# Prefix sums of a bucket sort on VectorE: adds with two bf16 operands become adds that take a float32 row or a PSUM scratch

## The chip, the cores and the metric

The kernel runs on one core of a Trainium2 chip. Times are device microseconds of one execution. The engines are named as the profile names them: PE (matmuls), PEld (its weight loads), DVE (VectorE), ACT (ScalarE), POOL (GpSimd, which here issues the indirect DMAs), SP (the queue of the plain DMAs).

## What is computed

One layer of message passing over a graph of 12,500 nodes with 64 features and 800,000 edges with 16 features each:

```python
def reference(x, e_attr, src, dst, w_msg, w_upd):
    N, D = x.shape
    m_in = jnp.concatenate([x[src], x[dst], e_attr], axis=-1)
    msg = _silu(m_in @ w_msg)
    agg = _segment_sum(msg, dst, N)
    return _silu(jnp.concatenate([x, agg], axis=-1) @ w_upd)
```

The edges come in random order. The kernel sorts them into 128 buckets of 98 destination nodes, and then works bucket by bucket.

## The kernel before

**Tables.** At the start `tables` multiplies the nodes with the two node parts of `w_msg`. The source part goes to DRAM as `A_d`, the destination part stays in SBUF as `BW`, one block for each bucket, with the edge part of the weights below it.

**Sorting, a step of eight tiles.** A tile is 128 edges, one on each partition. A `Step` takes M = 8 tiles, in two halves of ZB = 4. `Step.onehot` (ACT) makes `hf`, a float32 one-hot row of 128 buckets for each edge and tile. `Step.sums` (DVE, L397 to L408) adds these rows up over the tiles into `G[:, a, k, :]`, in bf16: for the half a, entry k is the sum of its tiles 0 to k. `Step.count` (PE) turns `hf` and `G` into counts, by products with triangular and all-ones matrices, into the PSUM tile `z`. `Step.ranks` (DVE, L429) reads from it each edge's place among the edges of its bucket in the chunk. `Step.expand` (DVE, L438 to L442) compares the places with slot numbers into `hit` and writes each edge's record into its slot of `X`; `Step.move` (PE, L459, then ACT, L464) sums the records of a chunk into the block `blk`, one row for each bucket. `Chunk.place` (DVE, L477, L478) moves the pointers on, and `Chunk.scatter` (POOL, L482) writes the block to DRAM with one indirect DMA.

**Chunks and turns.** The first K8 = 140 chunks have 8 tiles, one step each (`c.turn` = 3). From then on a chunk has C = 12 tiles, so that three steps hold two chunks, and `c.turn` runs through 0, 1, 2. There are 782 steps: 140 of turn 3, and 214 each of the turns 0, 1 and 2. In a chunk of 12 tiles a half can begin with tiles of its chunk already counted. The sum of these is the carry, `c.before(a)`: for the half a = 1 it is entry 3 of half 0 of the same step, for a = 0 it is entry 3 of half 1 of the step before. Entry 3 of a half is needed only where the chunk goes on after it. In turn 0 that is so for both halves, and half 1 takes a carry; in turn 1 for half 1, which begins a chunk; in turn 2 for half 0, with a carry; in turn 3 for half 0, without one.

**Messages, a batch of eight tiles.** Once enough sorted records lie in DRAM, a `Group` loads 64 tiles of them by plain DMAs, and a `Batch` of 8 tiles takes `gather` (POOL, L645: one indirect DMA for each tile, which reads 128 row numbers from `sidx` in SBUF and fetches 128 rows of `A_d` into one of four buffers `g`), `onehot` (DVE, L655, from `ioB`), `transpose` and `product` (PE, L664 and L673), `message` (DVE, L677: adds the product to the gathered rows, and so waits for the gathers; then ACT, L678), `reduce` (PE, L694) and `add` (DVE, L706).

**Order.** Every engine's queue is in the order in which `period` writes it. One period holds one stage each of a few steps and batches: the gathers of a batch with a scatter between their halves; `onehot` of a step and of the batch; the counts of the step before; the transposes; the reduction of an older batch; the ranks; `message` of an older batch; `add`; `sums` of the newest step; `expand` of the one before; `move`; the product; `place`. So on DVE a period runs L655, L429, L677, L706 twice, L403 twice, L405, L408 (in turns 0 and 2), L438, L439, L442 four times, L477, L478. POOL takes the gathers of a batch two periods before `message` needs them.

**Scratch in PSUM.** The tile `cb` is one bank of PSUM, 512 float32 wide on each partition. Before the change its columns 0 to 127 hold `ioB` (bucket-local node numbers, of which L655 reads 98), 128 to 157 `ioS`, and 256 to 495 `hit`.

Of the kernel before, what the change touches and what calls it, by code (L numbers as in the profile page):

```python
# [7 lines left out]
OP = mybir.AluOpType  # L8
# [6 lines left out]
P = 128  # L15
NBK = 128
BK = 98
# [5 lines left out]
M = 8  # L23
# [3 lines left out]
S = LIM[-1]  # L27
# [21 lines left out]
def mpnn_kernel(tc, x, e_attr, src, dst, w_msg, w_upd, out):  # L49
    nc = tc.nc  # L50
# [22 lines left out]
    with es:  # L73
# [22 lines left out]
        iof = cp.tile([P, P], F32, name="iof")  # L96
# [23 lines left out]


        cb = pc.tile([P, 512], F32, name="cb")
        ioB = cb[:, 0:P]
        ioS = cb[:, P:P + S]
        hit = cb[:, 2 * P:2 * P + M * S].rearrange("p (k s) -> p k s", s=S)
        nc.vector.tensor_copy(ioB, iof)
        nc.vector.tensor_scalar(out=ioS, in0=iof[:, 0:S], scalar1=RK, scalar2=None, op0=OP.add)


# [247 lines left out]
        class Step:  # L377
# [12 lines left out]
            def onehot(c):  # L390
                c.hf = hp.tile([P, M, NBK], F32, name="hf")

                for k in range(M):
                    nc.scalar.activation(c.hf[:, k, :], iof, AF.Square, bias=c.hi[:, k:k + 1])  # L394
                nc.scalar.activation(c.hf, c.hf, AF.Relu, bias=ones, scale=-1.0)  # L395

            def sums(c):  # L397

                c.G = tp.tile([P, 2, ZB, NBK], BF16, name="G")
                h = c.hf.rearrange("p (a k) b -> p a k b", k=ZB)  # L400
                nc.scalar.activation(c.G[:, :, 0, :], h[:, :, 0, :], AF.Copy)
                for k in (1, 2):
                    nc.vector.tensor_tensor(out=c.G[:, :, k, :], in0=h[:, :, 0, :] if k == 1 else c.G[:, :, k - 1, :], in1=h[:, :, k, :], op=OP.add)  # L403
                a, b = ((0, 2), (1, 2), (0, 1), (0, 1))[c.turn]
                nc.vector.tensor_tensor(out=c.G[:, a:b, 3, :], in0=c.G[:, a:b, 2, :], in1=h[:, a:b, 3, :], op=OP.add)  # L405
                if c.turn in (0, 2):
                    a = 1 if c.turn == 0 else 0
                    nc.vector.tensor_tensor(out=c.G[:, a, 3, :], in0=c.before(a), in1=c.G[:, a, 3, :], op=OP.add)  # L408

            def before(c, a):  # L410

# [204 lines left out]
        class Batch:  # L616
# [35 lines left out]
            def onehot(t):  # L652
                i0, n = t.i0, t.n
                t.q = qp.tile([P, BT, KQ], F32, name="q")
                nc.vector.tensor_tensor(out=t.q[:, 0:n, 0:BK], in0=ioB[:, None, 0:BK].to_broadcast([P, n, BK]), in1=t.grp.lo[:, i0:i0 + n, None].to_broadcast([P, n, BK]), op=OP.is_equal)  # L655
                nc.scalar.activation(t.q[:, 0:n, BK:KQ], t.grp.rt[:, i0:i0 + n, 0:DE], AF.Copy)

            def transpose(t, step):
# [109 lines left out]
        class Draws:  # L768
# [34 lines left out]
            def take(d, u, units):  # L803
                for f, done in zip(d.free(u), d.done):
                    left = units
                    for b in range(NB):
                        n = min(f[b], left)
                        done[b] += n
                        left -= n
# [118 lines left out]
        for k in range(0, NCH, 512):  # L928
            n = min(512, NCH - k)
# [8 lines left out]
        while work["used"] < large or (work["forming"] and work["forming"][-1].k < 2):  # L938
            b = take()
# [66 lines left out]
        while work["used"] < whole or lasts or work["cur"] is not None or work["forming"]:  # L1006
            b = take()
# [47 lines left out]
        with tc.If(more > 0):  # L1055
# [4 lines left out]
            with tc.If(nover > 0):  # L1060
# [12 lines left out]
                for k in range(0, NCH, P):  # L1073
                    n = min(P, NCH - k)
# [13 lines left out]
                with tc.For_i(0, nover, 1):  # L1088
# [36 lines left out]
                    def block(rs=None):  # L1125
                        for c in halves:
                            c.expand(rs)
                            e = c.move()
                        return e


                    c = block()
# [4 lines left out]
                    with tc.For_i(0, rounds, 1):  # L1137
                        c = block(rs)
# [36 lines left out]
```

## Time and profile before

| | us |
|---|---|
| runs of the kernel before | 8925.74, 8929.77, 8931.5 (median 8929.77) |
| the profiled execution, its time | 8929.85 |
| the span of its trace | 8928.0 |
| DVE busy in the span | 7216.6 |
| ACT busy | 5054.3 |
| POOL busy | 6599.6 |

How to read a profile of this kind: a busy time counts the engine's instructions alone. POOL's issue of an indirect DMA is shown as some 0.94 us of work and 0.30 us in which it is idle and waits for nothing that the profile shows, and this pair repeats. A row of a view that groups instructions gives line, engine, operation, output and inputs, shapes, count, then busy time and mean length, then the idle time of the engine just before them with what ended it. A row of the timeline gives the start and the length of one instruction, both in us from the start of the span. A row of a view by windows gives a stretch, its length, and for each engine the busy time in it with the number of instructions.

### The profile page before, as it was taken

To read this page: it belongs to the slowest core of one execution; us is meant where nothing else is said; L and a number is where in the kernel's file an instruction comes from. 1 tells how busy PE (TensorE), PEld (TensorE's weight loads), DVE (VectorE), ACT (ScalarE), POOL (GpSimd) and SP (SyncE) were. 2 spreads that over 40 slices of the span, in tenths; PEclk is the share of its full clock that TensorE was granted. 3 is DMA by queue.
4 is the path that set the end of the run, shared out by engine and by line. 5 is a ranking of instruction groups with operands and counts; after the bars stand their busy time and mean duration, and the time that the engine had idled before them with its cause. 6 is when DMAs were issued, how large, how long until landed. Compare 5 with 4: busy or idle time off the path is not lost. (4 is left out here: it accounts for less than half of the span.)

```text
span 8928.0 us, 155380 instructions
## 1 busy us (share of the span) xinstructions
PE 8156.2 (91%) x49053; PEld 5873.2 (66%) x49816; DVE 7216.6 (81%) x15722; ACT 5054.3 (57%) x12594; POOL 6599.6 (74%) x6908
## 2 busy tenths in 40 slices
PE   8899999999999999999999999999999999999767
PEld 5677776666666666666666666666666666666656
DVE  8999998888888888888888888888888888887233
ACT  7666666555555555555555555555555555555222
POOL 1677777777777777777777777777777777777776
PEclk9999999999999999999999999999999999999566
DMA  4222222222222222222222222222222222222323
GB/s 109 56 62 60 60 61 58 50 57 54 54 56 50 57 52 56 52 56 52 56 52 56 56 52 52 55 57 52 56 52 56 52 56 55 52 57 49 59 48 51
DMA packets 662901, 501.14 MB, mean 56 GB/s; under 512 B 492983, under 2 KB 529911, under 8 KB 662071
## 3 DMA queue, kind: packets, MB, share of 16 engines
q0 software_dynamic: 238976, 349.72, 16.8%
q1 hardware_dynamic: 422775, 141.27, 7.3%
q8 instruction: 401, 6.57, 0.3%
q14 instruction: 429, 3.51, 0.1%
q10 hardware_dynamic: 320, 0.07, 0.0%
HBM read 330.05 MB, written 152.30 MB: 54 GB/s over the span
## 5 line engine op out<-in xcount | busy, mean ns | idle before, releaser
L645 POOL DMA_INDIRECT g<-A_d,sidx x6322 | 6020.1, 952 | 1946.6 <-issue 1546.2
L459 PE MATMUL pl<-X,hf 128*128 128x291 f32 (+5 forms) x12512 | 4255.3, 492 | 6.2 <-DVE LOST L477 6.2
L459 PEld LDWEIGHTS pl<-X,hf 128*128 128x128 f32 x12512 | 2389.5, 198 | 1333.1 <-issue 842.5
L442 DVE TENSOR_TENSOR X<-cb,rec 128x442 f32<-128x442 f32 (+5 forms) x3128 | 2646.9, 908 | 26.7
L394 ACT ACTIVATE hf<-iof,shi 128x128 f32<-128x128 f32 x6256 | 1908.3, 389 | 872.9 <-PE pl L459 872.6
L673 PEld LDWEIGHTS pre<-w,qt 114*128 114x128 f32 x10496 | 1338.1, 202 | 580.7 <-issue 562.8
L673 PE MATMUL pre<-w,qt 114*128 114x64 f32 x10496 | 1343.6, 284 | 249.0 <-DVE g L677 247.3
L677 DVE TENSOR_TENSOR g<-pre,g 128x512 f32<-128x512 f32 (+1 forms) x818 | 548.9, 671 | 1191.7 <-DMA g<-A_d,sidx 769.4
L678 ACT ACTIVATE g<-g 128x512 f32<-128x512 f32 (+1 forms) x818 | 501.6, 613 | 1761.5 <-DVE g L677 1759.7
L694 PE MATMUL ag<-q,g 128*64 128x98 f32 x12644 | 775.8, 264 | 250.4 <-DVE wl L549 146.1
L429 DVE TENSOR_REDUCE rank<-z 128x8 f32<-128x1024 f32 x782 | 949.1, 1214 | 57.3 <-PE z L424 36.3
L395 ACT ACTIVATE hf<-hf,ones 128x1024 f32<-128x1024 f32 x782 | 899.1, 1150 | 25.4
L667 ACT ACTIVATE qt<-tq 114x1024 f32<-114x1024 f32 (+1 forms) x818 | 797.2, 975 | 156.5 <-PE tq L664 154.2
L664 PE MATMUL tq<-ident,q 128*114 128x128 f32 x6322 | 871.5, 283 | 14.3 <-ACT nodes L194 13.0
L694 PEld LDWEIGHTS ag<-q,g 128*64 128x64 f32 x12644 | 613.3, 143 | 411.5 <-issue 200.6
L664 PEld LDWEIGHTS tq<-ident,q 128*114 128x114 f32 x6322 | 766.9, 140 | 136.5 <-ACT nodes L194 20.5
L482 POOL DMA_INDIRECT st<-blk,ptrs x567 | 572.9, 1010 | 321.2 <-issue 141.1
L655 DVE TENSOR_TENSOR q<-cb,lo 128x784 f32<-128x784 f32 (+1 forms) x818 | 767.4, 938 | 2.2
L464 ACT ACTIVATE blk<-pl 128x512 f32<-128x512 f32 (+1 forms) x568 | 323.8, 570 | 782.9 <-PE pl L459 609.7
L706 DVE TENSOR_TENSOR ACC<-ag,ACC 64x98 f32 x1938 | 497.5, 257 | 108.6 <-PE ag L694 28.8
L422 PE MATMUL z<-G,onesb 128*128 128x384 bf16 x1564 | 511.4, 327 | 73.5 <-DVE G L403 13.7
L673 PE MATMUL pre<-BW,qt 114*128 (+1 forms) x2148 | 311.8, 305 | 109.4 <-DVE g L677 108.6
(137 smaller groups left out, 5099.1 us busy)
## 6 DMA issues: line engine op xcount, KB each, us to landing
g<-A_d,sidx POOLq DMA_INDIRECT x6322
ea<-in_e_attr SPq DMA_DIRECT2D x260, 192.0 KB
rt<-st SPq DMA_DIRECT2D x1312, 34.0 KB
st<-blk,ptrs POOLq DMA_INDIRECT x567
rt<-st SPq DMA_DIRECT2D x434, 8.5 KB
nodes<-in_x SPq DMA_DIRECT2D x62, 98.0 KB
ACC<-rt SPq DMA_DIRECT2D x11, 544.0 KB
rt<-st SPq DMA_DIRECT2D x320, 17.0 KB
```

Of the source, the lines that this page charges most:

```text
L394: nc.scalar.activation(c.hf[:, k, :], iof, AF.Square, bias=c.hi[:, k:k + 1])
L395: nc.scalar.activation(c.hf, c.hf, AF.Relu, bias=ones, scale=-1.0)
L429: nc.vector.tensor_reduce(out=c.rank, in_=c.z, axis=AX.X, op=OP.max)
L442: nc.vector.tensor_tensor(out=c.x[:, k:k + 2, 2:2 + n * R].rearrange("p k (s c) -> p k s c", c=R), in0=hit[:, k:k + 2, 0:n, None].to_broad ...
L459: nc.tensor.matmul(pl[:, 0:w], c.hf[:, k, :], c.x[:, k, 0:w], start=(n == (c.size - 1 if whole else 0)), stop=ends, skip_group_check=True)
L482: i = nc.gpsimd.indirect_dma_start(out=st, out_offset=bass.IndirectOffsetOnAxis(ap=c.ptr, axis=0), in_=c.blk[:, 2:], in_offset=None)
L645: j = nc.gpsimd.indirect_dma_start(out=t.g[:, i, :], out_offset=None, in_=A_d, in_offset=bass.IndirectOffsetOnAxis(ap=t.grp.sidx[:, k:k + ...
L655: nc.vector.tensor_tensor(out=t.q[:, 0:n, 0:BK], in0=ioB[:, None, 0:BK].to_broadcast([P, n, BK]), in1=t.grp.lo[:, i0:i0 + n, None].to_broa ...
L664: nc.tensor.transpose(t.tq[0:KQ, j * P:(j + 1) * P], t.q[:, j, :], ident)
L667: nc.scalar.activation(t.qt[:, 0:w], t.tq[0:KQ, 0:w], AF.Copy)
L673: nc.tensor.matmul(t.pre[:, i * D:(i + 1) * D], t.qt[:, i * P:(i + 1) * P], w, start=True, stop=True)
L694: o = nc.tensor.matmul(t.ag[t.half(v), v // 2 * BK:(v // 2 + 1) * BK], t.g[:, i, :], t.q[:, i, 0:BK], start=(k == 0), stop=(k == u - 1))
```

## The change

Only `Step.sums`, the layout of `cb` and the one reader of `ioB` are touched.

```diff
-        ioB = cb[:, 0:P]
-        ioS = cb[:, P:P + S]
-        hit = cb[:, 2 * P:2 * P + M * S].rearrange("p (k s) -> p k s", s=S)
-        nc.vector.tensor_copy(ioB, iof)
+        ioB = cb[:, 0:BK]
+        ioS = cb[:, BK:BK + S]
+        hit = cb[:, P:P + M * S].rearrange("p (k s) -> p k s", s=S)
+        nc.vector.tensor_copy(ioB, iof[:, 0:BK])
+        Gs = cb[:, P + M * S:2 * P + M * S]
...
-                a, b = ((0, 2), (1, 2), (0, 1), (0, 1))[c.turn]
-                nc.vector.tensor_tensor(out=c.G[:, a:b, 3, :], in0=c.G[:, a:b, 2, :], in1=h[:, a:b, 3, :], op=OP.add)
-                if c.turn in (0, 2):
-                    a = 1 if c.turn == 0 else 0
-                    nc.vector.tensor_tensor(out=c.G[:, a, 3, :], in0=c.before(a), in1=c.G[:, a, 3, :], op=OP.add)
+                for a in ((0, 1), (1,), (0,), (0,))[c.turn]:
+                    k = c.G[:, a, 2, :]
+                    if a == (1 if c.turn == 0 else 0) and c.turn in (0, 2):
+                        nc.vector.tensor_tensor(out=Gs, in0=c.before(a), in1=h[:, a, 3, :], op=OP.add)
+                        nc.vector.tensor_tensor(out=c.G[:, a, 3, :], in0=Gs, in1=k, op=OP.add)
+                    else:
+                        nc.vector.tensor_tensor(out=c.G[:, a, 3, :], in0=k, in1=h[:, a, 3, :], op=OP.add)
...
-                nc.vector.tensor_tensor(out=t.q[:, 0:n, 0:BK], in0=ioB[:, None, 0:BK].to_broadcast([P, n, BK]), in1=t.grp.lo[:, i0:i0 + n, None].to_broadcast([P, n, BK]), op=OP.is_equal)
+                nc.vector.tensor_tensor(out=t.q[:, 0:n, 0:BK], in0=ioB[:, None, :].to_broadcast([P, n, BK]), in1=t.grp.lo[:, i0:i0 + n, None].to_broadcast([P, n, BK]), op=OP.is_equal)
```

In turn 0 entry 3 was made by two adds: one over both halves (256 elements, a bf16 and a float32 operand), and one of 128 elements that adds the carry, with two bf16 operands. Now there are three of 128 elements: entry 3 of half 0; the carry plus the float32 row of half 1's last tile, into the float32 scratch `Gs` in PSUM; and `Gs` plus the sum of the half's first three tiles. In turn 2 the two adds stay two: the carry plus the float32 row into `Gs`, and `Gs` plus the sum. The instructions of turns 1 and 3 are the same as before. `ioS` and `hit` move to lower columns of the same bank, so that `Gs` has room.

## The prediction

> **What bounds the kernel now.** I read the page first, then the busy time by windows, then the waits of single engines, and last the timeline around the lines that change.
>
> ```profile
> span 8928.0 us, 155380 instructions
> PE 8156.2 (91%) x49053; PEld 5873.2 (66%) x49816; DVE 7216.6 (81%) x15722; ACT 5054.3 (57%) x12594; POOL 6599.6 (74%) x6908
> L645 POOL DMA_INDIRECT g<-A_d,sidx x6322 | 6020.1, 952 | 1946.6 <-issue 1546.2
> ```
>
> By busy share PE looks like the bound and POOL is only third. The windows over POOL say otherwise:
>
> ```profile
> 4000.00:6000.00 2000.00, 1516.65 (x1587) 0.97 0.23 54
> ```
>
> 1587 indirect DMAs leave 2000 - 1516.65 = 483.35 us idle, 0.305 us for each. That is the pause that the timeline below shows after every one of them, even with the next ready. So POOL never waits for another engine here: the gathers and scatters stand back to back, 1.25 us apart, and the kernel goes at their pace. DVE does wait, for the gathers' data (L677, from 1228 to 8250 us):
>
> ```profile
> L677 DVE TENSOR_TENSOR g<-pre,g 128x512 f32<-128x512 f32 x637 | 440.3, 691 | 899.6 <-DMA g<-A_d,sidx 587.0 <-issue 312.2
> ```
>
> 899.6 us over 637 periods is 1.41 us of slack in each. An edit on DVE is therefore worth only what it does to POOL's pace. The change touches turns 0 and 2 alone, which have one L408 each:
>
> ```profile
> L408 DVE TENSOR_TENSOR G<-G x428: 224/225/231, 1228.7 to 8212.9; 128x128 bf16<-128x128 bf16 x143
> ```
>
> So what counts lies between 1228.7 and 8212.9 us; a saving on POOL there moves everything behind it forward by as much, since POOL's gathers run on to 8906 us.
>
> **Where the two engines touch.** A gather behind which no sorting runs, and one in the sorted stretch:
>
> ```profile
> 4000.00:6000.00 2000.00, 1394.70 (x1465) 0.97 0.23 54
> 8300.00:8600.00 300.00, 226.80 (x241) 0.60 0.33 57
> ```
>
> 226.80/241 is 0.941 us for a gather in the tail, 1394.70/1465 is 0.952 us with sorting beside it: 0.011 us more in the mean. It is not spread evenly. This is a turn 0:
>
> ```profile
> 3010.46 0.94 POOL L645 DMA_INDIRECT g<-A_d,sidx  x1 [0.30 <-issue]
> 3011.71 1.16 POOL L645 DMA_INDIRECT g<-A_d,sidx  x1 [0.30 <-DMA g<-A_d,sidx]
> ...
> 3009.39 0.69 DVE L677 TENSOR_TENSOR g<-pre,g 128x512 f32<-128x512 f32 x1 [0.61 <-DMA g<-A_d,sidx]
> ...
> 3011.62 0.43 DVE L405 TENSOR_TENSOR G<-G,hf 128x256 bf16<-128x256 bf16 x1
> 3012.09 0.23 DVE L408 TENSOR_TENSOR G<-G 128x128 bf16<-128x128 bf16 x1
> 3012.23 0.17 DVE L438 TENSOR_TENSOR X<-rank,limc 128x8 f32<-128x8 f32 x1
> ```
>
> The gather of 3011.71 takes 1.16 us, 0.22 more than 0.94. L405 ends at 3012.05, 0.34 us after the gather's start. I read it so: some 0.12 us after its start (0.34 - 0.22) the gather reads its row numbers from SBUF, and where a VectorE add with both operands in SBUF is under way, it waits for that add's end. The converse happens too:
>
> ```profile
> 3043.33 0.46 DVE L403 TENSOR_TENSOR G<-hf 128x256 bf16<-128x256 f32 x1
> ...
> 3043.34 0.94 POOL L645 DMA_INDIRECT g<-A_d,sidx  x1 [0.30 <-issue]
> ```
>
> Here the gather starts 0.01 us after the add, is not lengthened, and the add takes 0.46 instead of 0.43. At 3011.62 against 3011.71, 0.09 us apart, the add won; the border lies between, and I take 0.04. L677, L706, L439 and L442 each have an operand in PSUM; the gather of 3010.46, which runs beside L677 and L706, keeps its 0.94.
>
> Turn 0 is hit most. Its chain of adds starts a fixed time after L677, L677 starts when a gather's data land, and so L405 meets a gather at nearly the same phase each time. Of the 214 turns 0, L405 lengthens a gather in 135. The windows laid on just these gathers, first those lengthened by over 0.13 us, then the others (first and last row, and the sum):
>
> ```profile
> 1404.52:1405.64 1.12, 1.12 (x1) 1.00 0.22 44
> 8190.77:8191.86 1.09, 1.09 (x1) 0.94 0.18 30
> sum 114.55, POOL 114.55; mean POOL 1.13
> ...
> 1568.53:1569.56 1.03, 1.03 (x1) 0.75 0.19 32
> 7829.76:7830.83 1.07, 1.07 (x1) 1.00 0.44 92
> sum 34.66, POOL 34.66; mean POOL 1.02
> ```
>
> The first group has 101 gathers, the second 34. Above 0.941 each they took 114.55 - 101 x 0.941 = 19.5 us and 34.66 - 34 x 0.941 = 2.7 us. The same for the 22 gathers of turns 0 that one of the two adds of L403 lengthens, and for all 147 that an add of L403 or L405 lengthens in turns 1 and 2:
>
> ```profile
> 1255.41:1256.46 1.05, 1.05 (x1) 1.00 0.71 230
> 8025.36:8026.51 1.16, 1.16 (x1) 1.00 0.13 28
> sum 23.73, POOL 23.73; mean POOL 1.08
> ...
> 1265.50:1266.46 0.96, 0.96 (x1) 1.00 0.46 153
> 8212.33:8213.32 0.99, 0.99 (x1) 1.00 0.13 31
> sum 151.33, POOL 151.32; mean POOL 1.03
> ```
>
> These are 23.73 - 22 x 0.941 = 3.0 us and 151.32 - 147 x 0.941 = 13.0 us.
>
> **The change, part by part.** The durations, from 1228 to 8250 us:
>
> ```profile
> L405 DVE TENSOR_TENSOR G<-G,hf 128x128 bf16<-128x128 bf16 x428 | 127.5, 298 | 14.7
> L405 DVE TENSOR_TENSOR G<-G,hf 128x256 bf16<-128x256 bf16 x214 | 92.1, 430 | 7.4
> L408 DVE TENSOR_TENSOR G<-G 128x128 bf16<-128x128 bf16 x428 | 96.4, 225 | 14.7
> L439 DVE TENSOR_TENSOR cb<-cb,rank 128x240 f32<-128x240 f32 x643 | 267.7, 416 | 8.4
> L706 DVE TENSOR_TENSOR ACC<-ag,ACC 64x98 f32 x1295 | 333.5, 258 | 56.4 <-issue 6.5 <-DVE g L677 1.3 <-PE pl L459 0.8
> ```
>
> *Turn 0, the wide add becomes a narrow one.* 430 ns become 298: the add begins where it did and ends 0.132 us sooner. Each of the 101 gathers that waited longer than that for its end saves 0.132, 13.3 us together; the 34 others start their read behind its end and save their 2.7 us. Sum 16.0 us. This is the whole of the gain that I can price.
>
> *Turn 0, the carry through the scratch (the first of two adds).* It has two SBUF operands and can itself hold up a gather. Its price is not in the trace. From below, L405's narrow form with like operands, 298; with L439, which writes PSUM, 416 less 112 elements at (430-298)/128 ns, it is 300. I take 298. From above 430, as if each element took twice as long. It starts 0.33 us behind the narrow add, 1.25 us into the chain, one gather's distance. A gather that it holds up, 0.04 to 0.18 us into it, thus follows one that started 0.04 to 0.17 us into the first L403; those are among the 22 above, and the wait is at most 298 - 40 - 120 = 0.14 us. Between nothing and 3 us; I take 0.4 us lost.
>
> *Turn 0, scratch plus sum.* One operand is in PSUM, as in L706, so it holds up nothing. L706's 258 plus 30 elements more makes 289 ns.
>
> *Turn 2.* The first add has the place and the operands' kind of the old L405, 298 ns; the second now has a PSUM operand and no longer holds up a gather, but the old L408, 225 long, hardly could: only one starting 40 to 105 ns into it. I take nothing. If the scratch add needed 430 ns, turn 2 would come to be what turn 0 was with its wide add, and lose some 16 us: the gain would be gone.
>
> *DVE's own time.* Behind L405 came L408 and L438, 0.61 us from L405 to L438 in the turn 0 above. After, two starts of 0.33 us and the last one 0.21:
>
> ```profile
> 3023.12 0.29 DVE L405 TENSOR_TENSOR G<-G,hf 128x128 bf16<-128x128 bf16 x1
> 3023.33 0.17 DVE L438 TENSOR_TENSOR X<-rank,limc 128x8 f32<-128x8 f32 x1
> ```
>
> That makes 0.87, 0.26 us more; in turn 2 it is 0.33 + 0.21 = 0.54 against 0.47 (3033.42 to 3033.89 below), 0.07 more. Behind it on DVE stand L438 to L478, and for these PE's moves, ACT's copy and the scatter. 214 x 0.33 = 71 us of DVE work in all, which I cost at nothing: the wait of 1.41 us ahead of L677 takes it in. If that cover were gone, it would be 71 us.
>
> *Layout of `cb`.* Columns move within one bank that DVE alone uses; the copy of `ioB` runs once. Nothing.
>
> **Sum.** 16.0 - 0.4 = 15.6 us, 8929.85 - 15.6 = 8914.3 us; the profiled execution lies 0.08 us above the median of the runs, so nothing is to be corrected. I predict 8914.
>
> **Rivals.** *The add with two bf16 operands is what blocks.* L408 takes 225 ns where L405 takes 298 for as many elements, so it runs in a faster mode, and it is what the change removes everywhere. If its mode held POOL up, all that turn 0 loses would vanish, 19.5 + 2.7 + 3.0 = 25 us, and of the 13.0 us of turns 1 and 2 some part: 8892 to 8905, say 8899. [...] The trace does not agree; a turn 2:
>
> ```profile
> 3033.28 0.94 POOL L645 DMA_INDIRECT g<-A_d,sidx  x1 [0.30 <-DMA g<-A_d,sidx]
> ...
> 3033.42 0.29 DVE L405 TENSOR_TENSOR G<-G,hf 128x128 bf16<-128x128 bf16 x1
> 3033.74 0.23 DVE L408 TENSOR_TENSOR G<-G 128x128 bf16<-128x128 bf16 x1
> 3033.89 0.16 DVE L438 TENSOR_TENSOR X<-rank,limc 128x8 f32<-128x8 f32 x1
> ```
>
> L408 lies wholly inside this gather, which keeps its 0.94; and at 3011.71 the delay ended with L405, before L408 began; turn 1 has no L408, and gathers are lengthened in it too. Chance 0.07.
>
> *The phase does not hold.* If the longer chain changes when L677 starts, gathers would meet the adds at any phase. Then an add of length d costs (d - 0.16)²/(2 x 1.25) in the mean: in turn 0 the wide add's 0.029 and L408's 0.002 become two narrow ones of 0.008, a gain of 0.015 x 214 = 3.3 us, 8926. For it: a later DVE could shift landings. Against it: L677 waits for data that POOL's pace sets. Chance 0.13.
>
> *The longer chain comes on the path.* Slower: if L677 no longer waits, every turn 0 and 2 pays for itself, 71 - 15.6 = 55 us, 8985. It decides from the point where the 0.26 us exceed L677's wait (0.61 us even in the short one above) so often that POOL finds its four buffers occupied. No pause of POOL speaks for it. Chance 0.13.
>
> **How the numbers follow.** The forecast has 0.67. Within it the gain is 15.6 give or take 4. A change of under 0.2%, 17.9 us here, is about what a measurement of this kernel can hardly tell from none. Of the forecast 0.32 lies beyond it and 0.35 within; the blocking bf16 add gives 0.07 faster, the lost phase 0.12 within, the longer chain 0.13 slower and 0.01 of the lost phase. Faster 0.39, same 0.47, slower 0.14. The range goes from the bf16 rival, 8899, to a scratch add of 430 ns, which leaves 8930, with 2 us for the spread of the runs: 8898 to 8932. Outside it lie the longer chain and a part of the bf16 rival, some 0.16.
>
> **What would show it.** Right: POOL still idles 0.305 us behind each DMA; in turn 0 the gathers that meet the third add are at most some 0.13 us longer than 0.94; the mean gather from 4000 to 6000 us falls from 0.952 to about 0.949; the scratch add takes about 298 ns and L677 still waits for gathers. Wrong: a scratch add of well over 300 ns, gathers held up beside the last add with its PSUM operand, a POOL pause over 0.4 us, or another phase of L677 against the gathers.

## The result and the profile after

Over 22 runs the changed kernel took 8913.85 us in the median (8909.3 to 8928.35), the kernel before in its 22 runs 8930.86 (8925.74 to 8934.1). The ratio is 0.9982, with a 95% interval of 0.9975 to 0.9988: 17.0 us less.

The page of the changed kernel:

```profile
span 8926.6 us, 155594 instructions
PE 8140.7 (91%) x49053; PEld 5860.1 (66%) x49816; DVE 7239.5 (81%) x15936; ACT 5057.0 (57%) x12594; POOL 6596.0 (74%) x6908
L648 POOL DMA_INDIRECT g<-A_d,sidx x6322 | 6016.1, 952 | 1949.0 <-issue 1541.8
```

This execution is the slowest of the 22, 8928.35 us, and by its span alone nothing seems gained. The reason is in the shortest and the median length of a gather, here first in the kernel before and then in the changed one (instructions of one line; min/median/max in ns, first and last start):

```profile
L645 POOL DMA_INDIRECT g<-A_d,sidx x6322: 940/944/1342, 203.4 to 8906.5; - x198
```

```profile
L648 POOL DMA_INDIRECT g<-A_d,sidx x6322: 941/947/1307, 205.7 to 8905.8; - x198
```

The median gather, which meets nothing, is 3 ns longer in this execution. 6322 x 0.003 us is 19 us, more than what separates the execution from the median of the runs (14.5 us). In f2_wide_kept and f4_reorder_after below, which have the same scratch add and last add, the median gather is 944 again; so the 3 ns belong to that execution and not to the change. What the change did is therefore read inside the execution, against its own 0.947.

POOL still stands back to back. The windows over all of its instructions, and then over the gathers alone:

```profile
4000.00:6000.00 2000.00, 1515.83 (x1588) 0.97 0.23 54
...
4000.00:6000.00 2000.00, 1393.56 (x1466) 0.97 0.23 54
```

(2000 - 1515.83)/1588 is 0.305 us of pause, as before. The mean gather is 1393.56/1466 = 0.951 us, which is 0.004 over the 0.947 of this execution's median; before it was 0.952, 0.008 over 0.944.

The adds and the wait for the gathers, from 1228 to 8250 us, grouped by line and shape:

```profile
L680 DVE TENSOR_TENSOR g<-pre,g 128x512 f32<-128x512 f32 x637 | 440.2, 691 | 874.9 <-DMA g<-A_d,sidx 559.9 <-issue 314.6
...
L408 DVE TENSOR_TENSOR cb<-G,hf 128x128 f32<-128x128 bf16 x428 | 127.2, 297 | 7.3
L411 DVE TENSOR_TENSOR G<-G,hf 128x128 bf16<-128x128 bf16 x428 | 127.2, 297 | 14.7
L409 DVE TENSOR_TENSOR G<-cb,G 128x128 bf16<-128x128 f32 x428 | 124.7, 291 | 14.7
```

L411 is entry 3 without a carry, L408 the scratch add, L409 scratch plus sum. L680 (L677 of before) still waits for gathers, 874.9/637 = 1.37 us a period.

A turn 0 in the changed kernel, DVE and then POOL:

```profile
3012.31 0.42 DVE L404 TENSOR_TENSOR G<-G,hf 128x256 bf16<-128x256 bf16 x1
3012.77 0.29 DVE L411 TENSOR_TENSOR G<-G,hf 128x128 bf16<-128x128 bf16 x1
3013.09 0.30 DVE L408 TENSOR_TENSOR cb<-G,hf 128x128 f32<-128x128 bf16 x1
3013.42 0.29 DVE L409 TENSOR_TENSOR G<-cb,G 128x128 bf16<-128x128 f32 x1
3013.63 0.16 DVE L441 TENSOR_TENSOR X<-rank,limc 128x8 f32<-128x8 f32 x1
...
3012.90 0.98 POOL L648 DMA_INDIRECT g<-A_d,sidx  x1 [0.30 <-DMA g<-A_d,sidx]
3014.18 1.00 POOL L485 DMA_INDIRECT st<-blk,ptrs  x1 [0.30 <-issue]
```

The gather starts 0.13 us into L411 and is lengthened, as the old one was by L405; but L411 is over 0.29 us after its start, and so the gather loses 0.03 us where the one quoted before lost 0.22. L411 lengthens a gather in 96 turns 0. The windows on these gathers, first, last and sum:

```profile
1232.14:1233.16 1.02, 1.02 (x1) 1.00 0.77 229
8188.62:8189.65 1.03, 1.03 (x1) 1.00 0.22 48
sum 96.90, POOL 96.90; mean POOL 1.01
```

96.90 - 96 x 0.947 = 6.0 us. The wide add cost 22.2 us by the prediction's 0.941, and 21.8 by the median of 0.944: 114.55 + 34.66 - 135 x 0.944. From L411 to L441 it is 0.86 us, 0.25 more than from L405 to L438 before.

### The profile page after: what moved, and what is told of

It is laid out like the page before. It is cut to its first block, busy times and chain, and to the rows that moved or that the text cites. A ratio compares the mean times of both kernels' runs of the same rounds, so it can differ in the third digit from the quotient of the medians.

```text
span 8926.6 us, 155594 instructions
## 1 busy us (share of the span) xinstructions
PE 8140.7 (91%) x49053; PEld 5860.1 (66%) x49816; DVE 7239.5 (81%) x15936; ACT 5057.0 (57%) x12594; POOL 6596.0 (74%) x6908
## 5 line engine op out<-in xcount | busy, mean ns | idle before, releaser
L680 DVE TENSOR_TENSOR g<-pre,g 128x512 f32<-128x512 f32 (+1 forms) x818 | 548.9, 671 | 1170.9 <-DMA g<-A_d,sidx 781.1
L681 ACT ACTIVATE g<-g 128x512 f32<-128x512 f32 (+1 forms) x818 | 501.6, 613 | 1724.0 <-DVE g L680 1720.4
```

## The experiments

The theory: POOL's pace sets the time; a gather reads its row numbers some 0.12 us after its start, and if an add with two SBUF operands is under way then, it waits for that add's end; the change gains because turn 0's wide add, which lengthened a gather in 135 of 214 turns 0, becomes one that is 132 ns shorter (430 and 298 ns before). The 0.12 us are an estimate from the trace of the kernel before: those 135 gathers end 0.82 us behind the add's end, and an undisturbed one takes 0.944. That it is the reading of the row numbers that waits is the author's reading; no trace shows what a gather does inside its 0.94 us. Below, a gather's "read" is the moment 0.12 us after its start. The main rival: the add with two bf16 operands is what blocks. A second one: the longer chain of adds has a price.

Six kernels were run, each on two chips. On the chip of the runs with e and g in their names the kernel before itself took 10,813 and 10,830 us, and POOL's pace was not its bound (the trace of e1_split below), so that these runs answer another question. Times in us, each beside runs of the kernel before on the same chip:

| kernel | time | before | difference | ratio, 95% interval |
|---|---|---|---|---|
| e1_split | 10817.73 | 10812.7 | +5.0 | 1.0005, 0.9996 to 1.0014 |
| e2_wide_kept | 10805.08 | 10812.7 | -7.6 | 0.9996, 0.9987 to 1.0005 |
| e3_reorder_before | 10795.13 | 10812.7 | -17.6 | 0.9988, 0.9978 to 0.9997 |
| e4_reorder_after | 10803.28 | 10812.7 | -9.4 | 0.9995, 0.9986 to 1.0004 |
| f1_split | 8919.64 | 8932.89 | -13.3 | 0.9984, 0.9975 to 0.9993 |
| f2_wide_kept | 8928.16 | 8932.89 | -4.7 | 0.9996, 0.9987 to 1.0005 |
| f3_reorder_before | 8908.74 | 8932.89 | -24.2 | 0.9974, 0.9965 to 0.9984 |
| f4_reorder_after | 8906.62 | 8932.89 | -26.3 | 0.9971, 0.9960 to 0.9982 |
| g5_all_wide | 10824.37 | 10830.0 | -5.6 | 0.9998, 0.9989 to 1.0006 |
| g6_long_chain | 10883.41 | 10830.0 | +53.4 | 1.0055, 1.0042 to 1.0068 |
| h5_all_wide | 8966.28 | 8942.28 | +24.0 | 1.0027, 1.0016 to 1.0037 |
| h6_long_chain | 8927.87 | 8942.28 | -14.4 | 0.9983, 0.9974 to 0.9992 |

### The wide add split, the bf16 carry kept

```diff
-                nc.vector.tensor_tensor(out=c.G[:, a:b, 3, :], in0=c.G[:, a:b, 2, :], in1=h[:, a:b, 3, :], op=OP.add)
+                for k in range(a, b):
+                    nc.vector.tensor_tensor(out=c.G[:, k, 3, :], in0=c.G[:, k, 2, :], in1=h[:, k, 3, :], op=OP.add)
```

> The kernel before, with one edit: turn 0 makes entry 3 of its two halves by two adds of 128 elements in place of one of 256; the carry is still added by an add with two bf16 operands, and there is no scratch. Theory (a gather that comes while an add with two SBUF operands is under way waits for that add's end, and the wide add of turn 0 is the one met most): nearly the whole gain is here, 16 us less than before, 8913 to 8917, and the gathers beside turn 0's adds lose some 9 us in all in place of 25. Rival (the add with two bf16 operands blocks): no gain, 8929 to 8932.

On the slower chip the difference of +5.0 us cannot be told from none, and the trace of e1_split shows why the gathers' length could not matter there. The waits of POOL from 1228 to 8250 us (waited for: total, times, longest), and DVE's add of the gathered rows (L678 there) in the same stretch:

```profile
POOL g L646 <- issue: 1133.1, 3465, 9.1
POOL g L646 <- remote: 960.1, 423, 3.2
...
L678 DVE TENSOR_TENSOR g<-pre,g 128x512 f32<-128x512 f32 x504 | 343.2, 681 | 0.0
```

POOL pauses for some 2.3 us (960.1/423) in most batches, and the add of the gathered rows is never waited into: its idle time is 0.0. The gathers are early there, and DVE would not notice one that is 0.2 us longer. There was next to nothing to shorten either: in g5_all_wide, on the same chip and with turn 0 as before, the wide add of turn 0 lengthens 3 gathers, by 0.1 us in all. "remote" means that the profile does not know what ended the pause, and what makes that chip slower is open.

> The same kernel as e1_split, on another chip: on the first one the kernel before took 10812.7 us and POOL had pauses of some 2.4 us in most batches, so POOL's pace set nothing there. Where the kernel before takes some 8930 us, theory: 8913 to 8917, and turn 0's adds cost the gathers beside them some 9 us in all in place of 25. Rival (the add with two bf16 operands blocks): 8929 to 8932.

f1_split took 8919.64 us, 13.3 less than the kernel before: without the scratch and with the bf16 add in place the larger part of the change's 17.0 is there (two comparisons, each with its own runs of the kernel before). The time is 3 us above the band of the theory. Windows on the 84 gathers that a narrow add lengthens in turns 0:

```profile
1230.51:1231.57 1.06, 1.06 (x1) 1.00 0.76 224
8083.65:8084.65 0.99, 0.99 (x1) 1.00 0.16 33
sum 83.95, POOL 83.95; mean POOL 1.00
```

83.95 - 84 x 0.944 = 4.7 us there. With the gathers that meet turn 0's first two adds all of turn 0 loses 12.7 us, not the 9 of the expectation.

### The wide add kept, no bf16 add left

```diff
                 for a in ((0, 1), (1,), (0,), (0,))[c.turn]:
                     k = c.G[:, a, 2, :]
+                    if c.turn == 0 and a == 0:
+                        nc.vector.tensor_tensor(out=c.G[:, :, 3, :], in0=c.G[:, :, 2, :], in1=h[:, :, 3, :], op=OP.add)
+                        continue
```

> The changed kernel, with one edit: turn 0 keeps the wide add of 256 elements over both halves; the scratch add and the last add then write half 1's entry again. No add has two bf16 operands any more. Theory: the gathers wait for the wide add as before, so the gain of turn 0 is gone: 8927 to 8932. Rival (the add with two bf16 operands blocks): its removal is what gains, so 8905 to 8915, as fast as the change or faster.

On the slower chip the difference of -7.6 us cannot be told from none.

> The same kernel as e2_wide_kept, on another chip. Where the kernel before takes some 8930 us, theory (the wide add of turn 0 is what the gathers wait for): 8927 to 8932. Rival (the add with two bf16 operands blocks, and none is left here): 8905 to 8915.

f2_wide_kept took 8928.16 us, with an interval that includes no change: what the theory gives, and far from the rival's 8905 to 8915. The 145 gathers that the wide add lengthens in turns 0 of f2_wide_kept:

```profile
1255.24:1256.28 1.03, 1.03 (x1) 1.00 0.51 98
8187.44:8188.48 1.03, 1.03 (x1) 1.00 0.13 32
sum 155.62, POOL 155.62; mean POOL 1.07
```

155.62 - 145 x 0.944 = 18.7 us, four times the 4.7 of the narrow add on the same chip. The rival falls. So does the new layout of `cb` as a source of the gain, since f2 has it too. The 4.7 us that the median lies below the kernel before may be noise or a small part of the change's gain (13.3 + 4.7 = 18.0, the change has 17.0); the interval does not tell them apart.

### The same adds at another time

Here `expand` is cut in two: `slots` holds the two instructions of L438 and L439, which find each edge's slot, and runs between the adds that make entries 1 and 2 and those that make entry 3. Every add is as it was. First in the kernel before, then in the changed one:

```diff
+                if between:
+                    between.slots()
                 a, b = ((0, 2), (1, 2), (0, 1), (0, 1))[c.turn]
...
-                h.sums()
+                h.sums(z)
```

> The kernel before, with the two small instructions that find each edge's slot (limit and hit, one SBUF operand that counts) moved ahead of the add or adds that make entry 3; every add stays as it was, wide and bf16 ones too. Entry 3 begins some 0.4 us later against L677. Theory: the phase at which a gather's read meets the chain is what costs; gathers cluster 0.95 to 1.2 us behind the chain's start, where now no add with two SBUF operands runs. Of the 38 us lost beside the adds some 9 remain: 8930 - 29 = 8901, between 8896 and 8910. Rival (what the operands are decides, not when they run): no change, 8929 to 8932.

> The same kernel as e3_reorder_before, on another chip. Where the kernel before takes some 8930 us, theory (the phase at which a gather's read meets the chain decides): 8896 to 8910, with every add as before. Rival (what the operands are decides): 8929 to 8932.

f3_reorder_before took 8908.74 us, 24.2 less than the kernel before, within the band, with the wide add and the bf16 add both in place. That is more than the 17.0 of the change, though the two were not timed side by side and their intervals overlap. A turn 0 of f3_reorder_before, DVE and then POOL:

```profile
3074.68 0.42 DVE L404 TENSOR_TENSOR G<-G,hf 128x256 bf16<-128x256 bf16 x1
3075.02 0.17 DVE L441 TENSOR_TENSOR X<-rank,limc 128x8 f32<-128x8 f32 x1
3075.20 0.42 DVE L442 TENSOR_TENSOR cb<-cb,rank 128x240 f32<-128x240 f32 x1
3075.53 0.41 DVE L408 TENSOR_TENSOR G<-G,hf 128x256 bf16<-128x256 bf16 x1
...
3075.39 0.94 POOL L652 DMA_INDIRECT g<-A_d,sidx  x1 [0.30 <-DMA g<-A_d,sidx]
```

The gather starts 0.19 us into L442, which has an operand in PSUM; the wide add starts 0.14 us behind the gather, after its read, and the gather keeps its 0.94 us. The wide add (L408 there) still lengthens 36 gathers in turns 0, but the windows on these sum to

```profile
sum 35.66, POOL 35.66; mean POOL 0.99
```

which is 35.66 - 36 x 0.944 = 1.7 us in all. The expectation left some 9 us lost; counted over all adds of `sums` in turns 0 to 2 it is 17.9, most of it beside the first two adds. (It also gave both moved instructions one SBUF operand that counts; L441 has both of its operands in SBUF, of 8 elements, and took 0.17 us above.)

On the slower chip the same kernel was 17.6 us faster, at an interval that just leaves out no change. Since POOL paces nothing there, the theory has no reason for it. It may be that X is begun earlier; no run here shows it. So the move may bring something of its own on the other chip too: the gathers account for 19.7 of the 24.2 us (table below).

> The changed kernel with the same move of the two small instructions ahead of the adds that make entry 3. Theory: some 9 us remain lost beside the adds, as in the kernel before with that move, so 8898 to 8906, some 13 us faster than the change, and equal to the other kernel with the move within 3 us: with the phase out of the way the change's own edits are worth next to nothing. Rival (operand types decide): 8914, no gain over the change.

On the slower chip the difference of -9.4 us cannot be told from none.

> The same kernel as e4_reorder_after, on another chip. Where the kernel before takes some 8930 us, theory: 8898 to 8906, within 3 us of the kernel before with the same move. Rival (operand types decide): 8914.

f4_reorder_after took 8906.62 us, 0.6 above the band, within 2.1 us of the kernel before with the same move, as the theory has it, and the fastest kernel of this study. It was not timed beside the change itself: against the kernel before it gains 26.3 us and the change 17.0, and the two intervals overlap by a little. In its turns 0 the third add lengthens no gather, and the scratch add one; what is left, 13.1 us over turns 0 to 2 where some 9 were expected, is lost almost wholly beside the first two adds.

### Longer adds in turns 1 and 2

```diff
-                a, b = ((0, 2), (1, 2), (0, 1), (0, 1))[c.turn]
+                a, b = ((0, 2), (0, 2), (0, 2), (0, 1))[c.turn]
```

> The kernel before, with turns 1 and 2 also taking the add over both halves (256 elements in place of 128; the entry made in vain is read by nobody). Theory (a gather waits for the end of the add that its read meets, so a longer add at the same place costs the gathers): turn 1 loses some 21 us in place of 7, turn 2 some 18 in place of 6; together 26 us more than the kernel before, 8952 to 8962 where that takes some 8931. Rival (only adds with two bf16 operands block; DVE has the time for 132 ns more): no change, within 3 us of the kernel before.

> The same kernel as g5_all_wide, on another chip. Where the kernel before takes some 8930 us, theory: 8950 to 8962, with some 20 us lost beside turn 1's adds and 18 beside turn 2's. Rival: within 3 us of the kernel before.

On the slower chip nothing changed; the longer adds of turns 1 and 2 lengthen 10 gathers there, by 0.7 us in all. On the other the kernel lost 24.0 us (8966.28 beside 8942.28; the expectation named the difference of 26 and a band of times for a chip that is some 12 us faster). Windows on the gathers that the wide add lengthens in h5_all_wide, 121 in turns 1 and then 113 in turns 2:

```profile
1268.04:1269.12 1.08, 1.08 (x1) 1.00 0.14 34
8237.68:8238.80 1.12, 1.12 (x1) 1.00 0.42 82
sum 129.53, POOL 129.53; mean POOL 1.07
...
1396.02:1397.17 1.16, 1.16 (x1) 1.00 0.15 35
8247.85:8249.02 1.17, 1.17 (x1) 1.00 0.13 28
sum 122.77, POOL 122.77; mean POOL 1.09
```

With that execution's median gather of 0.946 these are 15.1 and 15.9 us. The narrow add cost 4.2 us in turns 1 and 3.4 in turns 2 of the kernel before (57 gathers that sum to 58.00 us, and 51 that sum to 51.50, less 0.944 each). That is 23.4 us more on POOL for 24.0 measured: what an add costs the gathers comes out in the time nearly one to one.

### A longer chain that holds nothing up

```diff
-                        nc.vector.tensor_tensor(out=c.G[:, a, 3, :], in0=Gs, in1=k, op=OP.add)
+                        for _ in range(4):
+                            nc.vector.tensor_tensor(out=c.G[:, a, 3, :], in0=Gs, in1=k, op=OP.add)
```

> The changed kernel with the last add of turns 0 and 2 (scratch plus sum, one operand in PSUM) done four times in place of once: 428 times 3 x 0.33 us, some 420 us more of DVE work that holds no gather up by itself. Theory (POOL's pace sets the time and DVE waits 1.4 us a period for gathers): 8908 to 8922 where the change takes some 8914; the waits ahead of the add of the gathered rows shrink by most of the 420 us. Rival (DVE's chain is on the path): 40 us to 420 us more.

> The same kernel as g6_long_chain, on another chip. Where the kernel before takes some 8930 us, theory (the wait for the gathers takes the extra 420 us of DVE work in): 8908 to 8922. Rival (DVE's chain is on the path): 8950 and up.

On the chip where the kernel before takes 8942 us the lengthened kernel is still 14.4 us faster than it, and the change gained 17.0 beside its own runs of the kernel before; by the theory's bands the time is 6 us too high, and the kernel before beside it is 12 above the 8930 that the bands went by. Where the 420 us went, in h6_long_chain from 1228 to 8250 us:

```profile
L410 DVE TENSOR_TENSOR G<-cb,G 128x128 bf16<-128x128 f32 x1712 | 498.2, 291 | 58.3
...
L681 DVE TENSOR_TENSOR g<-pre,g 128x512 f32<-128x512 f32 x638 | 439.7, 689 | 449.9 <-DMA g<-A_d,sidx 261.4 <-issue 186.1
```

The wait ahead of L681 fell from 874.9 to 449.9 us, by 425. The extra work came out of the wait. On the slower chip, where e1_split shows no such wait, the same kernel lost 53.4 us, an eighth of the extra work; what hid the rest there is open.

## Why the prediction was right

**The bound.** Right: POOL's pace. POOL's pause is 0.305 us before and after, changes in the gathers' length come out in the time (h5), and 420 us of DVE work do not (h6). The whole set of traces says the same. For each, this is the time that gathers lose beside all adds of `sums` in turns 0 to 2, counted from the trace over the gathers that are more than 12 ns longer than that execution's median and end 0.80 to 0.84 us behind such an add, against the measured difference from the kernel before (us):

| kernel | lost beside the adds | less the kernel before | measured |
|---|---|---|---|
| before | 37.6 | | |
| the change | 18.1 | -19.5 | -17.0 |
| f1_split | 27.1 | -10.5 | -13.3 |
| f2_wide_kept | 35.7 | -1.9 | -4.7 |
| f3_reorder_before | 17.9 | -19.7 | -24.2 |
| f4_reorder_after | 13.1 | -24.5 | -26.3 |
| h5_all_wide | 62.3 | +24.7 | +24.0 |
| h6_long_chain | 18.2 | -19.4 | -14.4 |

Each row is one execution, and all stand against the one trace of the kernel before, which is not of the same runs as f and h; the two columns agree within 5 us.

**The mechanism.** Right in both parts, as far as lengths and times show it. That it is the wide add and not the bf16 add: f1 keeps the bf16 add and gains 13.3 us, f2 has none and gains nothing that can be told. That it is the time at which the add runs: f3 moves it and changes no operand, and gains 24.2. That the gather waits for the add's end: the 135 gathers that turn 0's wide add lengthens in the kernel before end 0.813 to 0.823 us behind that add's end, from 45 to 283 ns into the add as they began.

**The narrow add.** Predicted 16.0 us saved and so 22.2 - 16.0 = 6.2 left; measured 6.0 left, in 96 gathers where the prediction's grouping left 101. The longest of them is 0.12 us over the median of 0.947; 0.13 was the limit that the prediction set.

**The scratch add.** Taken at 298 ns, measured 297. It was to lose 0.4 us in turn 0; in the profiled execution it lengthened no gather of a turn 0. Scratch plus sum: 289 predicted, 291 measured, and it holds up nothing, as predicted: in the profiled execution 36 gathers come at least 45 ns into it with 20 ns or more of it left at their read, and none of them is more than 1 ns longer than the median.

**Turn 2.** Costed at nothing. All of turn 2 lost 5.7 us in the profiled execution of before and 3.5 in the one after. A difference of 2 us may be the phase of that execution: turn 1, whose instructions are the same, went from 7.2 to 5.8. The old carry add had no part in it there, since none of the 36 gathers whose read falls into L408 in turn 2 is more than 3 ns longer than the median. The 4.7 us of f2 stay open.

**DVE's longer chain.** 0.26 us more in turn 0 predicted, 0.25 measured, at no cost: the wait for the gathers fell only from 1.41 to 1.37 us a period. The cover is large but belongs to chips on which POOL paces; g6 shows the price without it.

**The rivals.** The blocking bf16 add falls with f1 and f2. The turn 2 that the prediction showed against it was weak evidence: L408 starts 0.46 us into that gather, well behind its read. The lost phase did not come: the third add of turn 0 still lengthens 96 gathers. The longer chain on the path falls with h6, on chips on which POOL paces.

**The signs.** All came but one as stated: the mean gather from 4000 to 6000 us was to fall from 0.952 to 0.949 and reads 0.951. It is the 3 ns of that execution; above the median it fell from 0.008 to 0.004, about as much as was forecast.

**What was a little off.** The prediction took the undisturbed gather as 226.80/241 = 0.941 us. A count by windows includes the gathers that the window's edges cut, and so the mean is too low; the median in the trace is 0.944. The 19.5 us of the first group are 19.2 by it.

**The sum.** 15.6 us predicted, 17.0 measured, 8914 against 8913.85. That the two agree so well is in part luck. The phase is that of one execution: in turns 0 of f1_split the first add lengthens 37 gathers and costs 7.6 us, in the kernel before as it was profiled 11 gathers and 1.9. That fits f1, which was forecast by the same sum and came out 3 us off.

## What to carry to other kernels

Look for the engine that never waits before the one that is busiest: POOL at 74% paced this kernel, PE at 91% did not. Here, where indirect DMAs paced the kernel, the VectorE adds with two operands in SBUF beside them had a price by their length (turn 0's third add cost the gathers 21.8 us at 430 ns, 6.0 as a narrow one) and their moment (1.7 us for the wide add in f3). Shortening the add gained 13.3 us in f1, and moving it so that it meets fewer reads 24.2 in f3, the most of the edits to the kernel before. Scratch plus sum, with an operand in PSUM, lengthened none of the 36 gathers that came into it; what such an operand gains by itself was not measured. An edit worth 0.2% is judged inside a trace by the lengths of the instructions that it was to change: the two profiled executions differ by 3 ns in the median gather, 0.944 and 0.947 us, and over 6322 gathers that is 19 us.

## What the runs showed of the hardware that was not expected

Where in a gather the delay arises can be told from the kernel before: some 0.12 us after its start, since a gather that turn 0's wide add lengthens ends 0.82 us behind the add's end and an undisturbed one takes 0.944. What counts there is which of the two starts first, with some 45 ns between: the gathers that come 45 ns or more into the wide add, with 15 ns or more of it left at their read, are all but four longer by more than 12 ns (135 of 139), and none that comes up to 44 ns into it is. Beside L706, an add with an operand in PSUM, no such delay shows: from 1228 to 8250 us 162 gathers of the kernel before come into it in the same way, and none is more than 9 ns longer than the median. The one gather of f3 quoted above keeps its 0.94 us while the wide add runs beside the rest of it, from 0.14 us on.

The adds with two bf16 operands, which take 225 ns where L405 takes 298 for as many elements, hold up no gather in these runs that the traces show: f1 keeps them and gains 13.3 us, f2 has none and gains nothing that can be told (4.7 us, with an interval that includes no change), and of 57 gathers of the kernel before that have a whole L408 inside them and whose read meets no other add of `sums`, none is longer (at most 5 ns over the median). Each gather whose read falls into an L408 had started before it, so what a bf16 add that is already under way would do is not shown.

The chips differed by more than any edit here: the same program took 8933 and 8942 us on two chips, and 10,813 and 10,830 in two sets of runs on a third. On the slow one PE's granted clock was 0.88 to 0.90, against 0.94 to 0.95 on the others. SP's register moves, 29 ns in the median, took over 200 ns in 384 of 2068 cases of e1_split and in none of f1_split, and in e1_split PE, ACT, DVE and POOL had pauses whose end the profile calls "remote". The cause stays open.
